# Narrow key products for the second step, halved copies in the first solve, and a new written-out order

## The chip, the cores and the metric

The kernel runs on one core of a Trainium2 chip. The metric is the device time of one execution in microseconds (us). The kernel before takes 895.24 us (median of 3 runs, 893.12 to 896.49). The core has five instruction streams that run beside each other and wait for each other by semaphores: PE (TensorE: matrix products and transposes, into PSUM banks), DVE (VectorE), ACT (ScalarE), POOL (GpSimd) and SP (which issues the DMAs). Each stream runs its own instructions in the order in which the program gives them.

## The reference

Three layers follow one another.

```
attention (B=4, H=8, S=768, D=48), a delta rule with one 48x48 state per batch and head:
    k_n = k / (|k| + 1e-6)
    for t in range(S):
        y[t]  = q[t] @ state
        state = state + beta[t] * outer(k_n[t], v[t] - state^T k_n[t])
x = y as [3072 tokens, 384]
first MoE-like layer:   h = x @ w_in (384 -> 2048);  g = relu(h)^2;  x = g @ w_out
second layer:           h = max(x @ w1, x @ w2, x @ w3) (384 -> 768);  out = h @ w_out2
```

## The kernel before

**Steps.** The 768 positions are cut into six steps of 128 (NS = 6, index t), each into two chunks of 64 positions (index c). In one step there are 16 pairs of heads (NP), so 32 units (NU: a pair and a chunk); a unit's two heads lie on partitions 0-63 and 64-127. Four batches (index b) of eight units make up a step.

**Per step** the kernel records these functions.

- `gram(t)`, line 464: for each batch the keys and the queries are transposed on PE (`features`) and copied from PSUM into the tile `W`; then `products` (line 483) multiplies each unit's keys with its keys (into bank `pk`) and with its queries (into bank `pq`). `pk` goes by ACT copies into the tile `G`; `pq` is multiplied by a triangular mask on DVE and goes back into `W`. For steps 1 and on the banks come from a ring of two (`gram_ring`), so that the transposes of the next batch wait until the copies and masks of this one have emptied the banks.
- For step 0 a key product is made as two products of 32 columns, one of them with its halves exchanged (`turned`), so that everything lands where `solve` wants it and one copy does (line 505). For the later steps it is one product of 64 columns, and up to four further small copies on ACT bring the quarters to their places (lines 506 to 511).
- `solve(t)`, line 551: from `G` a triangular inverse for each unit. DVE transposes `G` into `L`, runs two recurrences of 16 steps each (some 120 small dependent operations, tiles `T`, `Tn`), and transposes the result back into `Tn` and `G`. PE then makes two rounds of 32-by-32 products: `pm` (line 618), copied by ACT into `M1` (which is named L in the profile), and `pa`, `pb` (lines 629, 630). ACT copies these into `G` (line 635), ACT moves two blocks within `G` (line 638), and POOL clears the blocks from which they came (line 639).
- `chain(t)`, line 644: the recurrence over the two chunks, as alternating groups of small products and copies (`Removed`, `Updates`, `State`, `outputs`). `Updates` of chunk 0 in step 0 (line 677) is the first to read what `solve(0)` left in `G`.
- `moe1(t)`: the first layer for the step's 512 tokens, 16 blocks of `w_in` and `w_out`. In step 0 each weight block is also loaded and turned into a high and a low part (`load_w`: one DMA into one of two tiles `raw`, three operations on ACT and five on DVE through one tile `word`). `hidden` has one PSUM bank (`h_ring`), which ACT empties into `r`.

After the last step the second layer runs; it is not touched.

**Order.** Nothing is issued when it is recorded. A `Recorder` numbers every operation (products inside `together()` share a number) and `issue()` (line 229) emits them in the order of a list of numbers, `ORDER`, which has three parts: steps 0 to 4 with attention (3464 numbers), the end of the first layer (534) and the second layer (640). An engine's stream is what is left of the list when the other engines' numbers are struck out. So where an operation stands in the list decides what it can hold up on its own engine. Since `record` makes all calls, every row of the profile has line 247; rows are told apart by their tiles. A product of full 32-bit operands shows as two matmul instructions.

Of the kernel before, what the change touches and what calls it, by code (L numbers as in the profile page):

```python
# [11 lines left out]
AF = mybir.ActivationFunctionType  # L12
# [240 lines left out]
def kernel(  # L253
# [26 lines left out]
    pl = Recorder(nc)  # L280
# [183 lines left out]
    def gram(t):  # L464
# [66 lines left out]
        for keys in ((True, False) if t == 0 else (True,)):  # L531
            for b in range(B):
# [6 lines left out]
                nb = t * B + b + 2  # L539
                if nb < BLOCKS * B:  # L540
                    load_tok(nb // B, nb % B)
                products(slice(u0, u0 + 2 * HP), True, True)
        if t == 0:
            for b in range(2):
                load_tok(1, b)
# [494 lines left out]
```

## Time and profile before

| what | value |
|---|---|
| median of the runs | 895.24 us (893.12 to 896.49) |
| profiled execution | 894.54 us, span 892.8 us |
| PE busy | 858.6 us, 96% of the span |
| DVE busy | 535.7 us, 60% |
| ACT busy | 451.5 us, 51% |
| POOL busy | 35.0 us, 4% |
| mean granted TensorE clock | 0.965 of full speed |

The shares are means over stages with different limits. Slice by slice the page shows PE at six to nine tenths and at about half clock in the first four slices of 40 (the first 90 us), and at nine tenths or more and full clock in nearly all of the rest; DVE is at nine tenths or more in the first six slices except the first. The stretches in which PE waits are therefore to be looked for in the first 150 us.

### The profile page before, as it was taken

What the parts mean: (1) busy time and instruction counts of PE and PEld (TensorE: products, weight loads), DVE (VectorE), ACT (ScalarE), POOL (GpSimd) and SP (SyncE); (2) the same over time, 40 slices, a digit from 0 to 9 for tenths busy, and PEclk for the clock granted to TensorE, in tenths of its full rate; (3) what the DMA queues carried; (4) which work ended last, traced back from release to release, by engine and by line L of the source; (5) the groups of instructions that cost most, each with busy time, mean ns of one, the idle gap of its engine ahead of it and who ended that gap; (6) DMA issues with size and microseconds to landing.
All of it is one profiled execution on the core that took longest, in us unless ns stands there. A gap on an engine that the chain in (4) does not pass through costs nothing.

```text
span 892.8 us, 23837 instructions
## 1 busy us (share of the span) xinstructions
PE 858.6 (96%) x10284; PEld 717.2 (80%) x10284; DVE 535.7 (60%) x1185; ACT 451.5 (51%) x792; POOL 35.0 (4%) x55
## 2 busy tenths in 40 slices
PE   6678989999999999999999999999999999999998
PEld 4557976788887888888778888888988889898987
DVE  4999988799799689679543886325323141413131
ACT  5478778964655754665556896532222121312111
POOL 5010001000100100100000000000000000000000
PEclk8557999999999999999999999999999999999999
DMA  8456766576376347433434774420101000000000
GB/s 191 99 150 167 243 220 164 113 193 154 68 161 146 75 125 163 116 92 106 105 101 143 246 256 172 156 89 1 60 11 45 28 1 36 1 36 1 36 1 36
DMA packets 159785, 96.02 MB, mean 108 GB/s; under 512 B 129984, under 2 KB 133184, under 8 KB 159680
## 3 DMA queue, kind: packets, MB, share of 16 engines
q1 hardware_dynamic: 159168, 94.40, 38.3%
q8 instruction: 80, 1.31, 0.6%
q0 software_dynamic: 512, 0.10, 0.1%
q14 instruction: 25, 0.20, 0.1%
HBM read 79.53 MB, written 14.94 MB: 106 GB/s over the span
## 4 chain that ended last, share of the span: by engine, by line
PE 90%; DVE 6%; ACT 2%; DMA 1%; issue 1%; POOL 0%; SPq 0%; DVEq 0%; POOLq 0%; ACTq 0%
PE ps L247 90%; DVE Tn L247 1%; DVE word L247 1%; DMA raw<-in_moe_w_out_dram 1%; DVE W L247 1%; DVE T L247 1%; ACT G L247 0%; DMA kt<-in_k_dram 0%; ACT wo L247 0%; DVE wo L247 0%; ACT word L247 0%; DVE raw L247 0%; DVE L L247 0%; DVE US L247 0%; POOL G L247 0%
## 5 line engine op out<-in xcount | busy, mean ns | idle before, releaser
L247 PE MATMUL ps<-gh,wo 128*128 128x512 f32 (+1 forms) x624 | 161.4, 377 | 0.0
L247 DVE TENSOR_TENSOR r<-r,ps 128x512 f32<-128x512 f32 x72 | 49.4, 687 | 168.4 <-PE ps L247 167.9
L247 ACT ACTIVATE r<-ps 128x512 f32<-128x512 f32 (+1 forms) x140 | 80.0, 572 | 126.1 <-PE ps L247 122.6
L247 PEld LDWEIGHTS ps<-gh,wo 128*128 128x128 f32 x624 | 111.1, 188 | 21.0
L247 PE MATMUL ps<-xh,wih 128*128 128x512 f32 (+1 forms) x312 | 121.1, 388 | 4.2 <-ACT r L247 3.8
L247 PE MATMUL ps<-xh,wil 128*128 128x512 f32 (+1 forms) x312 | 116.6, 374 | 0.0
L247 PE MATMUL ps<-xl,wih 128*128 128x512 f32 (+1 forms) x312 | 116.5, 373 | 0.0
L247 DVE TENSOR_TENSOR gl<-r,gh 128x512 fp32r<-128x512 f32 (+1 forms) x104 | 66.6, 642 | 59.3 <-ACT gh L247 58.7
L247 PE MATMUL ps<-gl,wo 128*128 128x512 f32 (+1 forms) x312 | 83.4, 375 | 0.0
L247 PEld LDWEIGHTS ps<-xh,wih 128*128 128x128 f32 x312 | 58.6, 188 | 17.3 <-ACT r L247 5.6
L247 PEld LDWEIGHTS ps<-xl,wih 128*128 128x128 f32 x312 | 58.7, 188 | 10.8
L247 PEld LDWEIGHTS ps<-xh,wil 128*128 128x128 f32 x312 | 58.8, 188 | 9.0
L247 PEld LDWEIGHTS ps<-gl,wo 128*128 128x128 f32 x312 | 56.0, 188 | 10.7 <-DVE gl L247 0.3
L247 ACT ACTIVATE gh<-r 128x512 fp32r<-128x512 f32 (+1 forms) x104 | 61.6, 596 | 4.0 <-PE ps L247 1.8
L247 ACT ACTIVATE r<-r 128x512 f32<-128x512 f32 (+1 forms) x104 | 62.0, 597 | 2.4
L247 ACT ACTIVATE G<-ps 32x256 f32<-32x256 f32 (+3 forms) x116 | 51.3, 448 | 22.8 <-PE ps L247 21.0
L247 PE MATMUL ps<-W 64*64 64x64 f32 (+1 forms) x1664 | 49.3, 249 | 5.6 <-ACT W L247 3.5
L247 DVE TENSOR_TENSOR T<-T,Tn 128x96 f32<-128x96 f32 (+21 forms) x186 | 50.7, 273 | 2.1
L247 PEld LDWEIGHTS ps<-W 64*64 64x64 f32 (+1 forms) x1664 | 40.3, 151 | 13.6 <-issue 6.0
L247 ACT ACTIVATE raw<-ps 128x384 f32<-128x384 f32 (+1 forms) x32 | 16.5, 516 | 63.2 <-PE ps L247 63.1
L247 DVE TENSOR_TENSOR Tn<-L,T 128x96 f32<-128x96 f32 (+21 forms) x186 | 44.7, 271 | 0.8
L247 ACT ACTIVATE m1h<-r 128x512 fp32r<-128x512 f32 x18 | 11.4, 632 | 66.6 <-DVE r L247 66.6
(151 smaller groups left out, 1714.0 us busy)
## 6 DMA issues: line engine op xcount, KB each, us to landing
wo<-wod SPq DMA_DIRECT2D x88, 384.0 KB, 3.9
raw<-in_moe_w_out_dram SPq DMA_DIRECT2D x11, 768.0 KB, 5.4
raw<-in_moe_w_dram SPq DMA_DIRECT2D x9, 768.0 KB, 4.6
raw<-in_moe_w_in_dram SPq DMA_DIRECT2D x8, 768.0 KB, 5.0
wod<-wo SPq DMA_DIRECT2D x8, 768.0 KB, 5.4
out_dram<-raw SPq DMA_DIRECT2D x24, 192.0 KB, 1.8
x2d<-raw SPq DMA_DIRECT2D x12, 256.0 KB, 3.0
kn<-in_k_dram SPq DMA_DIRECT2D x14, 192.0 KB, 4.5
```

Of the source, the lines that this page charges most:

```text
L247: self.plan.add(lambda: fn(*args, **kw))
```

## The change

Four edits.

1. Step 1's key products are made as step 0's: two of 32 columns each in place of one of 64. The small copies behind them are not made in step 1.
2. In step 1 `products` is called twice per batch, first for the keys and then for the queries, so that a unit's key products and query products have numbers of their own and each group has its own bank and can stand anywhere in the order.
3. At the end of `solve`, the copies of `pa` (chunk 0) come ahead of those of `pb`; in step 0 the move within `G` and the clearing behind it are made chunk by chunk, four halves in place of two wholes.
4. The first two parts of `ORDER` are replaced (3484 and 534 numbers); the third is the same.

```diff
 ORDER = [
-29 32 4 0 24 28 1 27 25 26 5 30 2 3 1096 22 8 35 36 1119 37 38 7 49 324 39 50 51 52 40 167 53 163 63 64 41 21 42 43
...
-115 9 0 127 139 1 3 2 108 4 12 5 109 110 6 116 111 118 7 117 120 112 8 121 10 122 18 113 11 119 151 123 13 130 124
...
+115 0 9 139 1 3 2 4 108 151 5 109 127 110 6 118 111 116 7 117 120 112 8 121 10 122 18 113 11 119 123 13 128 12 163
...
@@ products
-                        if keys and t == 0:
+                        if keys and t < 2:
                             lo, hi = key[:, 0:32], key[:, 32:64]
                             turned = bass.AP(hi.tensor, hi.offset, [list(hi.ap)[0], [-32, 2], [1, 32]])
                             for o0, lhs, rhs in ((0, lo, key), (32, hi, turned)):
...
             if keys:
                 pl.scalar.activation(Gu, pk, AF.Copy)
-                for p0 in (32, 96) if t else ():
+                for p0 in (32, 96) if t > 1 else ():
                     p = slice(p0, p0 + 32)
                     pl.scalar.activation(Gu[p, :, 0:32], pk[p, :, 32:64], AF.Copy)
...
@@ gram
-                products(slice(u0, u0 + 2 * HP), True, True)
+                for which in ((True, False), (False, True)) if t == 1 else ((True, True),):
+                    products(slice(u0, u0 + 2 * HP), *which)
@@ solve
         Gc = G.rearrange("p (n c) k -> p c n k", c=2)
-        for p0 in (0, 64):
-            for c, px in enumerate((pa, pb)):
+        for c, px in enumerate((pa, pb)):
+            for p0 in (0, 64):
                 p = slice(p0, p0 + 32)
                 pl.scalar.activation(Gc[p, c, :, 32:64], px[p], AF.Copy, scale=-1.0)
-        for p0 in (32, 96):
-            p = slice(p0, p0 + 32)
-            pl.scalar.activation(G[p, :, 32:64], G[p, :, 0:32], AF.Copy)
-            pl.gpsimd.memset(G[p, :, 0:32], 0.0)
+        for cs in (slice(0, 1), slice(1, 2)) if t == 0 else (slice(0, 2),):
+            for p0 in (32, 96):
+                p = slice(p0, p0 + 32)
+                pl.scalar.activation(Gc[p, cs, :, 32:64], Gc[p, cs, :, 0:32], AF.Copy)
+                pl.gpsimd.memset(Gc[p, cs, :, 0:32], 0.0)
```

What the new list says of the first 135 us, read number by number against the recorded operations:

- **PE.** Ahead of the last key product of step 0 stand 16 transposes, where 18 stood. The products of step 1 come in alternating groups of four to sixteen narrow key products and two to eight query products. Counted by the shape of the part of the array that a product uses (all of it, 64 by 64, 64 by 32, 32 by 32), neighbours of unlike shape meet 68 times before the first `pm` product (35 before the change), 20 times from there to the first `Updates` product (11), and 28 times from there to the first product of `moe1` (24). Between the first `pm` product and the first `Updates` product stand 44 products of step 1's gram matrices (32 before); four query products of step 1 stand behind the first `Updates` product.
- **DVE.** The operations between the transpose into `L` and the transpose into `G` of step 0 are the same but for one more (a `word` operation of `load_w` that stood just ahead). Two masks of step 0's queries move forward in it. Between step 1's third and fourth pair of masks (in the profile those that begin at 50.09 and 57.15 us) stand a few more operations of the recurrence.
- **ACT.** The four halves of the move within `G` stand right behind the copy into `M1`; then come a copy of `G` for step 1, the `wih` copy of a weight block, and the two copies of `pa`. Near 130 us the squaring of `r` stands ahead of the `word` operation of the next weight block instead of behind it.
- **SP.** Step 0's queries and step 1's tokens are asked for earlier, step 0's values and chain keys later.

## Rows read from the trace of the kernel before

**Rows 1.** Busy time in stretches: window, us, PE, PEld, DVE, ACT, POOL, clock, DMA

```profile
17.75:60.51 42.76, 26.30 (x364) 20.54 (x364) 41.89 (x128) 23.86 (x43) 0.00 (x0) 0.54 0.60 143
60.51:71.32 10.81, 8.12 (x326) 6.51 (x324) 10.40 (x13) 8.00 (x13) 5.10 (x5) 0.50 0.37 113
71.32:80.20 8.88, 8.88 (x214) 8.13 (x214) 8.59 (x27) 7.60 (x15) 0.00 (x0) 0.50 0.55 171
80.20:120.00 39.80, 39.56 (x646) 37.65 (x641) 38.28 (x118) 30.09 (x66) 0.00 (x0) 1.00 0.71 208
120.00:150.00 30.00, 26.25 (x530) 20.58 (x532) 24.93 (x41) 23.32 (x38) 3.46 (x4) 1.00 0.60 187
150.00:893.00 743.00, 737.74 (x7954) 615.50 (x7946) 406.01 (x848) 349.25 (x607) 13.42 (x18) 1.00 0.34 94
```

**Rows 2.** What PE waited for over the span: us, times, longest

```profile
PE ps L247 <- DVE W L247: 9.8, 4, 3.3
PE ps L247 <- ACT r L247: 3.8, 4, 2.0
```

**Rows 3.** Timeline of PE, the last key products of step 0

```profile
15.37 1.71 PE L247 MATMUL ps<-W 64*32 64x64 f32 x53 [1.88 <-issue]
17.01 0.47 PE L247 MATMUL ps<-ident,r 128*128 128x128 f32 x1
```

**Rows 4.** Timeline of DVE, the solve of step 0

```profile
15.76 0.55 DVE L247 TENSOR_SCALAR word<-word 128x768 f32<-128x768 f32 x1
17.75 1.91 DVE L247 STREAM_TRANSPOSE L<-G 128x1024 f32<-128x1024 f32 x1 [1.44 <-ACT G L247]
...
57.15 0.64 DVE L247 TENSOR_TENSOR W<-ps,mask 64x512 f32<-64x512 f32 x1
...
58.53 1.98 DVE L247 STREAM_TRANSPOSE G<-T 128x1024 f32<-128x1024 f32 x1
```

**Rows 5.** ACT's groups by shape, 36 to 104 us: the small copies of step 1

```profile
L247 ACT ACTIVATE G<-ps 32x256 f32<-32x256 f32 x8 | 3.0, 375 | 0.2
...
L247 ACT ACTIVATE G<-ps 32x128 f32<-32x128 f32 x8 | 2.1, 263 | 0.1
```

**Rows 6.** Timeline of PE, one batch of step 1

```profile
50.84 0.90 PE L247 MATMUL ps<-ident,qt 128*128 128x128 f32 x3 [2.80 <-DVE W L247]
...
54.66 1.98 PE L247 MATMUL ps<-W 64*64 64x64 f32 x62 [0.61 <-ACT W L247]
```

**Rows 7.** Timeline of PE, products of unlike shape in turn

```profile
62.73 0.49 PE L247 MATMUL ps<-W 64*64 64x64 f32 x8
63.15 0.26 PE L247 MATMUL ps<-Tn,G 32*32 32x32 f32 x1
...
64.41 1.34 PE L247 MATMUL ps<-W 64*64 64x64 f32 x40
65.68 0.26 PE L247 MATMUL ps<-G,L 32*32 32x32 f32 x1
```

**Rows 8.** Timeline of PE, the end of solve(0) and the start of chain(0)

```profile
67.95 0.24 PE L247 MATMUL ps<-L,Tn 32*32 32x32 f32 x1
69.77 0.44 PE L247 MATMUL ps<-vn,G 64*64 64x48 f32 x2 [1.58 <-POOL G L247]
71.32 1.48 PE L247 MATMUL ps<-vn,G 64*64 64x48 f32 x23 [1.11 <-POOL G L247]
```

**Rows 9.** Timeline of ACT, and then of POOL, in the same stretch

```profile
69.69 0.91 ACT L247 ACTIVATE wih<-raw 128x768 fp32r<-128x768 f32 x1
70.63 1.20 ACT L247 ACTIVATE G<-ps 32x512 f32<-32x512 f32 x2
...
68.77 1.94 POOL L247 MEMSET G<- 32x1024 f32 x2 [0.61 <-ACT G L247]
```

**Rows 10.** Timeline of ACT, and then of PE, near 130 us

```profile
129.98 0.89 ACT L247 ACTIVATE word<-raw 128x768 f32<-128x768 f32 x1 [1.83 <-DMA raw<-in_moe_w_out_dram]
130.78 0.61 ACT L247 ACTIVATE r<-r 128x512 f32<-128x512 f32 x1
...
132.09 0.59 ACT L247 ACTIVATE r<-ps 128x512 f32<-128x512 f32 x1
...
132.74 0.50 PE L247 MATMUL ps<-xh,wih 128*128 128x512 f32 x1 [1.99 <-ACT r L247]
```

316 rows, old and new, of the table ORDER are left out of this document.

## The prediction

> **What bounds the kernel now.** First the busy time in stretches [rows 1], to see which engine fills which stretch. The reader is to see three regimes. From 17.75 to 120 us DVE is busy for 41.89 of 42.76 us, 10.40 of 10.81, 8.59 of 8.88 and 38.28 of 39.80: it is idle for only 0.9 + 0.4 + 0.3 + 1.5 = 3.1 us. PE is busy for 26.30 of 42.76 us in the first of these stretches, 8.12 of 10.81 in the second, and is full, with nothing to spare, from 71.32 to 120. From 120 to 150 PE is idle for 3.75 us. After 150 it is busy for 737.74 of 743 us: there nothing can be gained but by less work, and the change leaves none out. Then the waits of PE [rows 2]: what it waits for in front is DVE's masks (9.8 us in 4 times), and what it waits for later is ACT's `r` (3.8 us in 4 times). Then the timelines, at the places that the new list touches [rows 3 to 10]. The end is thus set by a chain: `solve(0)` on DVE, 17.75 to 60.51; its last products and copies on PE and ACT, to 71.32; PE to 120; and near 130 us the loading of weights, where ACT's `word` operation waits 1.83 us for a transfer, the copies of `r` stand behind it, and PE waits 1.99 us for `r` [rows 10].
>
> **The change part by part.**
>
> *The copies that go.* Eight of 375 ns and eight of 263 ns [rows 5], 5.1 us of ACT. ACT is busy for 23.86 of 42.76 us there [rows 1] and none of the four long waits of PE in that stretch is for it [rows 2]. I take 0; the ends are -5.1 (every one on the path) and 0.
>
> *The key products doubled.* 32 units times two heads are 64 more products, 128 more matmul instructions. What one costs comes from two runs of alike products: 8 between neighbours of another shape took 0.42 us (62.73 to 63.15) and 40 took 1.27 us (64.41 to 65.68) [rows 7]. So one costs (1.27 - 0.42)/32 = 0.027 us, and the rest, 0.21 us, comes once in each group, that is, once per change of shape. The last group of step 0, 53 in 1.64 us [rows 3], gives the same 0.027 with 0.2 left over. I take 0.19 a change, the ends being 0.16 and 0.21.
>
> [...]
>
> Where the changes of shape lie decides. (a) Before the first `pm` product there are 33 more (68 for 35): 6.3 us, and most of the instructions, on an engine that idles for 16.5 us in that stretch [rows 1]. They cost nothing as long as each batch is ready when DVE comes to its mask. The third batch is the tightest: PE restarts at 50.84 [rows 6] and the last query product comes some 5.8 us later; DVE masks at 57.15 [rows 4]. With 11 of the new changes and 32 of the new instructions it grows by 2.1 + 0.9 us, less 1.1 us, which key products fill while PE waits for `W` (0.61 of it in the row at 54.66 [rows 6]): 7.7 us. DVE's slot is 6.4 us and becomes some 7.05 with the operations moved into it. DVE then stands for 0.65 us, and behind that mask is the rest of the recurrence and the transpose into `G` at 58.53 [rows 4], for which everything waits. Ends: 0, and 3.3 (the longest wait in front [rows 2]). I take +0.65. (b) Between `pm` and chain(0) there are 9 more changes and some 24 more instructions: 1.7 + 0.65 = +2.35 us of PE. (c) From there to `moe1` 4 more and some 8 instructions: +1.0.
>
> *The start of solve(0).* Two transposes fewer stand ahead of the last key product; one is 0.90/3 = 0.3 us [rows 6]. DVE's transpose into `L` waits through ACT for these products [rows 4]: -0.6. Ends: -1.9, if the stall of 1.88 us ahead of them, which no wait explains ("issue" [rows 3]), went too, and +1.9 if it came twice.
>
> *The moved word operation.* 0.55 us [rows 4] goes from ahead of `solve(0)`, where DVE waits 1.44 us anyway, into it, where DVE is full: +0.55. The ends are 0 and 0.55.
>
> *The halves.* Before, the last `pa` product ends at 68.19 and chain(0) starts at 71.32 [rows 8], 3.13 us later, since ACT does the `wih` copy (69.69, 0.91 us) ahead of the last copies of `pa` and `pb` (70.63, 0.60 each), and POOL clears for 1.94 us [rows 9]. After, two copies of `pa` stand behind the product, 1.2 us and some 0.2 of passing on, with POOL's halves (0.49 each) beside them: 1.4, that is -1.7. The cover is the `wih` copy's being over by then; it now stands ahead of both copies. If it starts as late as 69.69, `pa` is copied by 71.8: +0.5, the other end.
>
> *The order near 130.* The squaring of `r` (0.61 us) ahead of the `word` operation that waits for a transfer [rows 10]: -0.6. Ends: -2.0, PE's whole wait, and 0.
>
> *The end of the first layer.* Another order of PE in a stretch where it is full [rows 1]: 0, within the 5.3 us that it idles after 150.
>
> The sum has two strands. PE alone would come to 120 us later by 2.35 + 1.0 - 1.7 = 1.65 us, beyond what DVE brings. But from 120 to 150 it idles for 3.75 us because the weights aren't there, and these are DVE's and ACT's work, which a late PE doesn't delay: the 1.65 are hidden. What isn't hidden is what moves DVE and the weights: -0.6 + 0.55 + 0.65 - 0.6 = 0.0. On the profile's 894.54 us (a span of 892.8 and 1.7 around it) that gives 894.6. The median of the runs is 0.7 above the profile, the lowest run 1.4 below it, so I add nothing.
>
> **The rivals.**
>
> *A. Faster: the front moves as a whole.* The stall of 1.88 us ahead of the last key products goes with the changed instruction stream, the tail of `solve(0)` gets its -1.7, and PE's wait near 130 gives 0.6: -4.2, 890.3. For it: the stall has no releaser in the trace [rows 3], and what starts `solve(0)` earlier moves DVE and the weights alike. Against it: the gain of the tail is PE's alone and would end in the wait for weights.
>
> [...]
>
> [...]
>
> *C. Slower: the drains outrun DVE's slots.* With 0.21 us a change and no key product that fills PE's wait for `W`, a batch of step 1 takes 5.8 + 2.3 + 0.9 = 9.0 us against a slot of 7.05, and DVE stands for 1.95 us at the last masks of each of three batches: +5.9, less the 0.65 that the sum has: 899.8, and with `pa` copied late (+0.5 instead of the tail's gain, PE then coming 3.9 us late to the 3.75 us of idling) 900. It decides as soon as a batch is over 7.05 us. For it: PE already stands at the masks (9.8 us [rows 2]) in a fixed cycle, each engine waiting in turn for the other. Against it: that PE waits there for DVE and not DVE for PE.
>
> *D. The change does nothing that the end sees*: both strands hidden, 895.2, the median.
>
> **How the numbers follow.** Forecast 0.36, D 0.12 (the two give no measurable change), A 0.16, B 0.14, C 0.22. About 0.5%, 4.5 us, is what a measurement of this kernel can tell from no change: faster is below 890.8, slower above 899.7. A and B lie just over that bound and would each fall short of it by a third of an us less, but with parts of the tail's or the start's gain beside them they reach 888; so I count 0.29 faster of their 0.30, and 0.21 slower of C's 0.22, whose miss goes to no change: 0.50. The likeliest one's own range comes from the ends of start (-1.9 for -0.6), order (-2.0 for -0.6) and DVE's wait (3.3 for 0.65): 892 to 897.5. To hold 8 in 10 the range takes in most of A and B (with the start's other end beside B, 890.1 - 1.3, about 888.5) and C to 900.5.
>
> **What would show it.** Right: no 32x256 and 32x128 copies of `G` in step 1; no idle DVE over 0.7 us ahead of a mask from 17 to 58; the transpose into `L` about 0.6 earlier and that into `G` within 1 us of 58.53; from the last 32-by-32 product to the first of `vn,G` some 1.4 us; PE full to 120 and then idle for about 2 us, in place of 3.75, up to 150. [...] DVE waiting for PE's products ahead of masks, two or three times over 1.5 us, says C. The forecast is wrong if PE's waits from 120 to 150 don't shrink when PE comes late, for then the weights hang on PE after all, and the 1.65 us count in full.

## The result and the profile after

The changed kernel takes 900.64 us (median of 6 runs, 898.0 to 903.07) beside 895.03 us for the kernel before (median of 6): 1.0063 times as long, 95% interval 1.0049 to 1.0078. A second set of runs of the same kernel (a_again, below) gave 899.58 us and 1.0050, 1.0033 to 1.0067. Slower, where no measurable change was forecast, and just outside the range of 888.5 to 900.5. The profiled execution has a span of 896.3 us; it is the quickest of the six (898.0 us), so its 3.5 us over the profile before are less than the medians' 5.6.

First, busy time cut at the same four events in both kernels: the transpose into `L`, the transpose into `G`, the second group of `vn,G` products (chain(0) under way), the first product of `moe1`, the end. Columns as in [rows 1]. The kernel before:

```profile
17.75:58.53 40.78, 24.34 (x353) 19.03 (x353) 39.91 (x128) 22.63 (x41) 0.00 (x0) 0.54 0.58 142
58.53:71.32 12.79, 10.08 (x335) 8.02 (x335) 12.37 (x14) 9.22 (x16) 5.10 (x5) 0.50 0.45 120
71.32:82.03 10.71, 10.47 (x287) 9.41 (x287) 10.03 (x32) 9.00 (x17) 0.00 (x0) 0.59 0.46 143
82.03:892.82 810.79, 801.96 (x9036) 672.45 (x9036) 467.78 (x1000) 401.26 (x707) 16.88 (x22) 1.00 0.37 103
```

The kernel after:

```profile
15.36:58.41 43.05, 32.97 (x447) 22.80 (x447) 40.65 (x128) 20.51 (x32) 0.00 (x0) 0.62 0.68 149
58.41:71.51 13.10, 11.92 (x352) 8.99 (x353) 12.14 (x15) 7.73 (x14) 3.40 (x6) 0.50 0.39 113
71.51:84.58 13.07, 11.83 (x295) 10.28 (x295) 11.04 (x25) 8.79 (x15) 2.25 (x3) 0.52 0.35 96
84.58:896.29 811.71, 802.59 (x9039) 674.08 (x9036) 468.85 (x1006) 396.90 (x706) 17.84 (x22) 1.00 0.38 103
```

`solve(0)` starts 2.4 us earlier, and loses 2.3 of them before it ends (43.05 for 40.78). The next stretch is 0.3 longer, the one to the first layer 2.4 longer, all the rest 0.9: together 3.5. PE is busy for 8.6 us more in the first stretch, DVE for only 0.7 more; so DVE has come to wait there. The timeline of DVE shows for whom (beside [rows 4], where no such wait stands):

```profile
15.36 1.93 DVE L248 STREAM_TRANSPOSE L<-G 128x1024 f32<-128x1024 f32 x1
...
36.64 0.68 DVE L248 TENSOR_TENSOR W<-ps,mask 64x512 f32<-64x512 f32 x1 [0.45 <-PE ps L248]
...
56.99 1.39 DVE L248 TENSOR_TENSOR W<-ps,mask 64x512 f32<-64x512 f32 x2 [1.06 <-PE ps L248]
58.41 1.94 DVE L248 STREAM_TRANSPOSE G<-T 128x1024 f32<-128x1024 f32 x1
```

PE in turn waits less for DVE's masks than the 9.8 us of [rows 2]; over the whole span it is now

```profile
PE ps L248 <- DVE W L248: 4.1, 3, 3.0
```

PE at the end of `solve(0)` and in chain(0), to be read beside [rows 8]:

```profile
69.90 0.24 PE L248 MATMUL ps<-L,Tn 32*32 32x32 f32 x1
70.90 0.41 PE L248 MATMUL ps<-vn,G 64*64 64x48 f32 x2 [0.76 <-POOL G L248]
71.51 1.91 PE L248 MATMUL ps<-vn,G 64*64 64x48 f32 x30 [0.20 <-POOL G L248]
74.66 1.94 PE L248 MATMUL ps<-vn,G 64*64 64x48 f32 x32 [1.24 <-issue]
```

The tail from the last `pa` product (ended at 70.14) to the chain is 1.37 us, as forecast. Then PE stands for 1.24 us in the midst of one group, for nothing that the profile names. The waits of PE from the first product of `moe1` to the end, columns as in [rows 2], before and after:

```profile
PE ps L247 <- ACT r L247: 3.8, 4, 2.0
```

```profile
PE ps L248 <- issue: 3.4, 5, 1.4
PE ps L248 <- ACT r L248: 1.2, 2, 0.7
```

The waits for `r`, 2.6 us of which the new order does away with, have been replaced by five that have no releaser. Before, there was one such wait, ahead of `solve(0)` [rows 3].

### The profile page after: what moved, and what is told of

Its sections match the earlier page's. It is cut to its first block, busy times and chain, and to the rows that moved or that the text cites. A ratio compares the mean times of both kernels' runs of the same rounds, so it can differ in the third digit from the quotient of the medians.

```text
span 896.3 us, 24087 instructions
## 1 busy us (share of the span) xinstructions
PE 869.6 (97%) x10412; PEld 724.6 (81%) x10412; DVE 537.8 (60%) x1185; ACT 443.3 (49%) x779; POOL 36.2 (4%) x57
## 4 chain that ended last, share of the span: by engine, by line
PE 93%; ACT 2%; DVE 2%; DMA 2%; issue 1%; SPq 0%; POOL 0%; ACTq 0%; DVEq 0%
PE ps L248 93%; DMA raw<-in_moe_w_in_dram 1%; DMA wod<-wo 1%; DVE W L248 1%; ACT W L248 1%; DMA wo<-wod 0%; ACT raw L248 0%; DVE G L248 0%; DVE L L248 0%; SPq L248 0%; ACT word L248 0%; ACT G L248 0%; ACT r L248 0%; ACT L248 0%; DVE Tn L248 0%
## 5 line engine op out<-in xcount | busy, mean ns | idle before, releaser
L248 PE MATMUL ps<-gh,wo 128*128 128x512 f32 (+1 forms) x624 | 163.4, 377 | 0.5 <-DMA wo<-wod 0.3
L248 PEld LDWEIGHTS ps<-gl,wo 128*128 128x128 f32 x312 | 55.9, 188 | 10.4
L248 PE MATMUL ps<-W 64*64 64x64 f32 (+1 forms) x1792 | 61.3, 251 | 2.5 <-ACT W L248 1.6
L248 ACT ACTIVATE G<-ps 32x256 f32<-32x256 f32 (+3 forms) x100 | 45.7, 469 | 31.4 <-PE ps L248 30.2
L248 PEld LDWEIGHTS ps<-W 64*64 64x64 f32 (+1 forms) x1792 | 46.5, 143 | 16.0 <-issue 8.8
L248 DVE TENSOR_TENSOR Tn<-L,T 128x126 f32<-128x126 f32 (+19 forms) x186 | 45.1, 271 | 0.9
L248 DVE TENSOR_TENSOR W<-ps,mask 64x512 f32<-64x512 f32 x48 | 33.0, 687 | 20.0 <-PE ps L248 19.3
```

Source lines behind the costliest of these rows:

```text
L248: self.plan.add(lambda: fn(*args, **kw))
```

## The experiments

Two theories at first. F: the waits without a releaser are waits for PE's own instructions. The traces have transfers of 16 KB each on an instruction queue, q8, here as the page of the profile after counts them (transfers, MB, share):

```profile
q8 instruction: 81, 1.33, 0.6%
```

That is one for each 128 of PE's 10412 matmul records or so. Each of the six waits begins within 2.1 us of the start of one, and ends 2.2 to 2.4 us behind that start. D: the loss is PE's added work, 64 products and the changes of shape. The pads move the instructions behind them against the blocks, at a place where PE waits anyway:

```diff
             for a in range(HP):
+                with pl.together():
+                    for _ in range(N if t == 0 and not keys and b == 0 and a == 0 else 0):
+                        pl.tensor.matmul(ps[0:32, 0, 0:64], ident[0:64, 0:32], ident[0:64, 0:64], start=True, stop=True)
                 pl.tensor.transpose(
```

**a_pad16, a_pad32, a_pad48** (N = 16, 32, 48).

> The changed kernel with 16 added products of 32 columns (32 matmul instructions more) at the first query transposes of step 0, where PE then waits 5 us anyway; they write a bank that the transposes overwrite. They move all later instructions of PE by 32 matmuls (and 32 weight loads) against the 16 KB blocks in which its instructions arrive. Theory F (fetches): the six waits of PE without a releaser in the profile after (4.6 us in all: 1.24 at 73.42, 1.41 at 141.13, 0.95 at 149.71 and three smaller; the kernel before has one, 1.88 at 13.49) are waits for such blocks, so they go or turn up at other work; their sum changes by over 1 us and the time with it (898 to 903). Theory D (drains): the loss is the 64 more products and the changes of shape; the waits without a releaser stay at the same work and the time at 900.6 within 0.7.

> As a_pad16 with 32 products (64 matmuls, half a block of 128). F: none of the six waits is left at the work where it was; a sum of such waits between 1 and 4 us elsewhere, and the time lower by what is missing to 4.6 (and by some 2 us more if the one at 73.42 goes, since the clock then rises earlier): 896 to 900. D: the same six waits, 900.6 within 0.7.

> As a_pad16 with 48 products (96 matmuls). F: the waits at other work again, the time differing from that of a_pad16 or a_pad32 by over 1 us. D: 900.6 within 0.7, as the others.

Measured: 911.23 us (1.0183 of before, 1.0159 to 1.0207), 902.81 (1.0099, 1.0082 to 1.0116) and 903.41 (1.0096, 1.0080 to 1.0112). D's 900.6 fails. F's direction holds and its sizes fail: the pads of 32 and 48 made it slower, not quicker, and a_pad16 left its range (its waits without a releaser come to 9.5 us, one of them 2.58 in chain(0), the clock was at half for two more stretches behind them, the mean over its profile 0.959 for 0.968, and POOL held DVE up, below). What speaks most for F is where the waits stand. Counting PE's matmul records from the start, the changed kernel stands without a releaser ahead of records 1112, 2260, 2388, 2643, 3026 and 5064. a_pad16, with 32 records more in front, stands ahead of 1113, 2260, 2388 and 3026 and four later ones; a_pad32, with 64 more, of 2260, 2388, 2516 and 2771 and others. Behind 130 us the counts stay, whatever the pad, and are multiples of 128 apart, but for a shortfall that grows to 21 by record 7871 (taken for records that the trace lacks); the work that stands there is another. Not every wait without a releaser is one of these. In chain(0), a_pad32 stands for 0.49 us ahead of record 1208, which is out of this step: there PE goes on at 75.64, 0.1 us behind the end of ACT's copy into `US`, which the next product reads.

**a_wide**: the four small copies stand right behind each copy of the bank.

```diff
-                        if keys and t < 2:
+                        if keys and t == 0:
...
-                for p0 in (32, 96) if t > 1 else ():
+                for p0 in (32, 96) if t else ():
```

> The changed kernel with step 1's key products of 64 columns again and the small copies on ACT back, each right behind the copy of its bank, all else in the new order. That takes out 128 matmul instructions, exactly one 16 KB block with their weight loads, so that from step 1's end on the blocks begin at the same work as in the changed kernel. D: the 3.5 us of instructions and the changes of shape that narrow products bring go, 896 or less. F: the waits at 141, 150 and 174 us stay, and the time falls by no more than 2 us: 898.5 to 901.

897.93 us (1.0041, 1.0025 to 1.0056), below F's range and above D's: both are in it. With 128 matmuls less the late waits stand ahead of records 2132, 2260, 2515 and 2898, 128 less each, and so at the same work: of the changed kernel

```profile
142.54 0.21 PE L248 MATMUL ps<-L,Tn 32*32 32x32 f32 x1 [1.41 <-issue]
150.66 0.62 PE L248 MATMUL ps<-W 64*64 64x64 f32 x25 [0.95 <-issue]
```

and of a_wide

```profile
143.68 0.21 PE L281 MATMUL ps<-L,Tn 32*32 32x32 f32 x1 [1.87 <-issue]
151.24 0.62 PE L281 MATMUL ps<-W 64*64 64x64 f32 x25 [0.36 <-issue]
```

**b_pad32, b_pad64**: the same in the kernel before, with products of 32 by 32 on the four diagonal blocks of `ident`; half a block and a whole one.

> The kernel before with 32 added products of 32 by 32 (64 matmuls, half of a 16 KB block of PE's instructions) ahead of the first query transpose of step 0, where PE waits 1.95 us for a transfer and DVE bounds the stretch. Their output is overwritten. Theory F (fetches): the kernel before has but one wait for a block because of where its blocks happen to begin; moved by half a block, it gets waits without a releaser behind 130 us as the changed kernel has, always at the same places in the count of matmuls, 1.5 to 8 us in all: 897 to 903. Theory D (drains): nothing has changed that costs: 894.6 within 0.7.

> As b_pad32 with 64 products (128 matmuls, a whole block), so that behind the pad the blocks begin at the same work as in the kernel before. F: no wait without a releaser behind 130 us, and what the pad itself costs is hidden or under 1.5 us: 894 to 896.5, below b_pad32 although it does twice as much. D: 894.6 to 896.5, and not below b_pad32.

903.06 us (1.0092, 1.0077 to 1.0106) for half a block, 895.05 (0.9997, 0.9988 to 1.0007) for a whole one, though the whole one is twice the work. From the first layer's start on PE waited in b_pad32

```profile
PE ps L247 <- issue: 6.1, 6, 1.4
PE ps L247 <- ACT r L247: 3.9, 4, 2.1
```

and in b_pad64

```profile
PE ps L247 <- ACT r L247: 4.8, 5, 2.2
PE ps L247 <- issue: 1.7, 1, 1.7
```

F is shown, for the waits and for what they cost here. Not all of its expectation came true: one wait of 1.7 us did come in b_pad64, and b_pad32 came just above its range. Besides its 6.1 us, the clock fell to half there for 3.4 us at 134 us, right behind a wait of 2.09 us for `r`; that is some 1.7 us more, if PE's work there would have taken half the time at full clock (an estimate).

**a_front, a_pool, a_front_pool, a_front_pool_wide, b_rest**: lists put together from the two. a_front is the changed kernel up to the first product of `moe1` and the old order from there; a_pool has POOL's first operations in their old order; the next two add these up, the last with wide products; b_rest is the old order up to that product and the new one from there. Of a_pool, POOL's numbers in the list (167, 168 and 34 clear `T`, `Tn` and `US`, the others issue transfers of beta):

```diff
-4 7 6 5 16 10 8 168 15 17 9 19 13 14 12 167 11 34 18
+4 7 6 5 167 16 10 8 15 17 9 19 13 14 12 11 18 168 34
```

> The changed kernel up to the first product of the first layer in the list; from there on, and in the list's second part, the order of the kernel before. All four edits of the code stay. The block phase is that of the kernel before (exactly one block more). F: the waits at 141, 150, 160 and 174 us (3.1 us) go, since other work stands where the blocks end there, the one at 73 stays: 896 to 898.5. D: the loss is made in the front and stays: 899.5 to 901.5.

> The changed kernel with POOL's operations of the first 14 us in the order of the kernel before: the clearing of T right behind the fourth transfer of beta, Tn and US last. The trace of a_pad16 shows a word operation of DVE that takes 4.1 us instead of 0.56, up to the end of POOL's clearing (14.16), and solve(0) starting 3.3 us late for it; in the profile after the same operation ended 0.6 us ahead of that clearing. Theory P: this is hit in a part of the runs of the changed kernel and makes their spread (898.0 to 903.1): here 898 to 899, and within 2.5 us of each other. Rival: POOL's order does nothing: 900.6 within 0.7, with the same spread.

> a_front with POOL's first operations in the order of the kernel before (as a_pool). F and P: no wait for a block behind 130 us, and no run in which solve(0) starts 3 us late; what is left is the front of the profile after, some 2.5 us late at the first layer for the wait at 73 us and the 9 more changes of shape ahead of chain(0): 896 to 897.5. If the order behind the front were no cause: 898.5 to 900.

> a_front_pool with key products of 64 columns in step 1 (as a_wide). Of the change that leaves the front's order, the separate banks and the halves. D's part, the price of the narrow products themselves, is the difference to a_front_pool: 1.5 to 3 us; so 893.5 to 895.5. If narrow products cost nothing: as a_front_pool.

> The kernel before up to the first product of the first layer in the list, and from there on (and in the second part) the order of the changed kernel; no edit of the code. F (fetches): the phase of the blocks is a whole block off that of the changed kernel, so the waits without a releaser at 141 to 174 us of its profile turn up here at the same work, 2.5 to 4.5 us: 897 to 900. D (the loss is in the front): 894 to 896.

Measured: a_front 899.54 us (1.0061, 1.0043 to 1.0080), a_pool 898.93 (1.0045, 1.0028 to 1.0062), a_front_pool 899.34 (1.0052, 1.0038 to 1.0066), a_front_pool_wide 897.0 (1.0032, 1.0020 to 1.0043), b_rest 894.87 (1.0003, 0.9991 to 1.0015). F's waits came and went where it said: none behind 80 us in a_front, 3.0 us in b_rest, at the work where the changed kernel has them. But F's times failed in both: b_rest is not slower, a_front hardly quicker. a_front_pool came where the rival to F and P had it. a_front_pool_wide missed its 893.5 to 895.5, but is 2.3 us under a_front_pool, inside D's 1.5 to 3; a_wide is 2.7 under the changed kernel. By the ratios the two differences are 1.8 and 2.0 us, with intervals that overlap a little. So narrow products make some 2 us in this front, and some 3 are left without them. From the first layer on the two orders take the same (811.71 and 810.79 us above, 812.35 in a_front_pool), the one with waits for blocks, the other with waits for `r`. The loss is ahead of the first layer. Of a_front_pool, again cut at the four events:

```profile
16.07:61.82 45.75, 35.70 (x447) 24.56 (x447) 40.66 (x128) 20.42 (x32) 0.00 (x0) 0.53 0.60 138
61.82:74.94 13.12, 11.93 (x353) 9.00 (x354) 12.15 (x15) 7.75 (x14) 2.84 (x5) 0.50 0.40 111
74.94:87.70 12.76, 11.45 (x295) 9.89 (x295) 10.60 (x25) 8.80 (x15) 2.64 (x3) 0.54 0.49 123
87.70:900.05 812.35, 802.78 (x9038) 672.68 (x9036) 468.93 (x1006) 401.62 (x706) 16.90 (x22) 1.00 0.37 102
```

and DVE in its `solve(0)`:

```profile
38.87 0.68 DVE L290 TENSOR_TENSOR W<-ps,mask 64x512 f32<-64x512 f32 x1 [1.68 <-PE ps L290]
...
49.54 0.69 DVE L290 TENSOR_TENSOR W<-ps,mask 64x512 f32<-64x512 f32 x1 [1.20 <-PE ps L290]
...
60.40 1.39 DVE L290 TENSOR_TENSOR W<-ps,mask 64x512 f32<-64x512 f32 x2 [1.10 <-PE ps L290]
```

In the five profiles with the old front and its products, pads and new late order included, the transpose into `G` starts 40.75 to 40.78 us behind that into `L`, DVE idle for 0.86 or 0.87 of them. In those with the new front it is 42.9 to 45.8, DVE idle for 2.2 to 5.1, mostly at masks. The new front leaves PE little slack there, so what PE's clock does in it now counts: DVE's idle time was 5.1 us where the granted clock of that stretch was 0.53 (a_front_pool), 3.9 to 4.0 at 0.55 and 0.56 (a_front, a_again, a_pad16), 3.5 at 0.59 (a_pool), 2.4 at 0.62 (after), 2.2 at 0.67 and 0.72 (a_pad32, a_pad48), while the kernel before ran at 0.54 with 0.9. With wide products it was 2.9 at 0.53 (a_front_pool_wide) and 2.5 at 0.56 (a_wide), so at like clock the narrow products are 1.4 to 2.2 us of it. All this goes with the wider spread of the runs; that it makes it is argued, not shown.

P (POOL) is a third thing. The new list moves POOL's first operations too, which the reading of the list ahead of the prediction left out. In a_pad16, timeline of DVE, then of POOL:

```profile
9.90 4.67 DVE L248 TENSOR_SCALAR word<-word 128x768 f32<-128x768 f32 x2 [7.84 <-ACT word L248]
```

```profile
11.04 0.97 POOL L248 MEMSET T<- 128x1024 f32 x1
11.94 0.62 POOL L248 DMA_DIRECT2D bl<-in_beta_dram  x1
12.55 1.61 POOL L248 MEMSET US<- 128x1792 f32 x1
```

The two `word` operations take 1.16 us where POOL's clearing comes behind them. Here the second (10.50 to 14.57) was running when the clearing of `T` began, and ended 0.4 us behind that of `US`; `solve(0)` began at 18.63 for 15.36. The operation was held so too in a_front (the two 4.68 us, `solve(0)` at 19.01) and in a_group (4.70 us, 18.16), and with POOL's old order in none. In all three the long operation lies beside two clearings and the issue between them and ends 0.4 us behind the second clearing, though here the one held had started first (10.50 for 11.04). No run shows what holds it. Not every operation of DVE is held: in the profile after, `SCALAR_TENSOR_TENSOR` (10.53, 0.96 us) ran as long as ever (28 of them take 0.95 in the mean) beside the clearing of `T` (11.07 to 12.04). There a `word` operation takes 1.63 us in chain(0) instead (72.60 to 74.23), beside POOL's clearings of `US` and `Tn` (71.96 to 73.81). a_pool's times don't show that P makes the changed kernel's spread: 895.8 to 901.2 is as wide as before.

**b_halves**: the old kernel with the halved copies of `solve(0)` alone (the loop over `cs` in the diff of the change). In the list both copies of `pa` stand ahead of `wih`: ACT's and POOL's numbers there, those of the halves in brackets,

```diff
-316 ... 314 ... 310 315 wih 317 312 311 ... 313
+[314 316] ... [318 320] ... 310 312 [315 317] wih [319 321] 311 ... 313
```

> The kernel before with the halved copies and clearings of solve(0) alone, both copies of pa ahead of the wih copy; PE's instructions are the same, so its blocks are too. The prediction's two strands: the tail from the last pa product to the first Updates group that follows on its clears shrinks from 3.1 to about 1.5 us, chain(0) starts 1.6 us earlier, and PE's waits between 120 and 150 us grow by as much: 894.2 to 895.5. Rival: PE's gain counts in full: 893.3.

895.06 us (1.0009, 0.9999 to 1.0019), as the two strands have it. But not by their reason: PE stood as long as ever near 130 us (2.00 us for `r`). The tail went from 3.1 to 2.4 us only, and the first layer began at 80.63, as in b_rest (80.75), for which the tail is the old one: the gain was lost within chain(0) (11.1 us from its second group to the first layer, 10.4 in b_rest).

**a_group, b_alt, b_sep, a_again**: what makes the batches too long, changes of shape (S) or the places (O)? b_alt has the first edit of the change alone, b_sep the first two, both in the old order. In a_group the key (K) and query (Q) products of a batch change places, as in the second batch:

```diff
-K K K K Q K K Q Q K Q Q Q Q K Q
+K K K K K K K K Q Q Q Q Q Q Q Q
```

> The changed kernel with the same places in the list for step 1's products, but in each batch the eight units' key products first and the eight units' query products behind them: some 7 changes of shape fewer in the second and third batch each, and fewer in the fourth; the number of products and everything else is the same. Theory S (slots: DVE stands in solve(0) because a batch of step 1 takes PE longer than DVE's work between two pairs of masks): a batch gets 1.3 us shorter, DVE's waits for products in solve(0) (2.4 us in the profile after, up to 5.1 in other runs of this front) fall under 1.5, 897.5 to 899.5. Rival O (the places of transposes and copies set these waits, not the changes of shape): 900.6 within 0.7.

> The kernel before with narrow key products in step 1 and without the small copies behind them, in its own order: each unit then runs two narrow products, a query product, two narrow ones, a query product, so a batch has 32 changes of shape more instead of 11 and 32 instructions more. S: 32 x 0.19 + 0.9 = 7.0 us more for a batch, 12.8 against a slot of 6.4: DVE stands for some 6 us at each of the last three pairs of masks, solve(0) takes 55 to 60 us instead of 40.8, 908 to 916. O, or a change of shape that costs less than the rows of the kernel before let it seem: under 900.

> b_alt with key and query products of a batch apart: eight units' keys, then eight units' queries, in the places where the old order has the units. Two changes of shape more a batch: 0.4 + 0.9 us, 7.1 at most against 6.4. S: solve(0) takes 41 to 43 us, 894.5 to 897. O: as b_alt, or as the kernel before within 0.7.

> The changed kernel once more, for a second profile. If its loss and its spread are made ahead of the first layer, the stretch from the first product of the first layer to the end is 811 to 813 us as in all kernels with blocks in this phase (810.8 in the profile before), and that product begins at 84 to 88 us, later by what solve(0) takes beyond 43 us. If they are made behind it: over 814.

a_group 897.7 us (1.0029, 1.0011 to 1.0047), b_alt 930.27 (1.0405, 1.0388 to 1.0423), b_sep 895.94 (1.0018, 1.0002 to 1.0034). DVE's waits for PE from 15 to 86 us, in a_group, b_alt and b_sep:

```profile
DVE W L281 <- PE ps L281: 1.7, 1, 1.7
```

```profile
DVE W L279 <- PE ps L279: 27.4, 3, 9.2
```

```profile
DVE W L280 <- PE ps L280: 3.2, 2, 2.3
```

b_alt shows the mechanism: the old order with alternating shapes, and DVE stands for 9 us at each of three pairs of masks; 6 were expected, so the price was taken too low. From the transpose into `G` to the last `pa` product PE took 17.2 us there for 7.7, which makes most of the rest of its 35. (In b_alt narrow key products also stand between the two heads' query products, where one of the same shape stood; the runs don't part the two.) b_sep's time is in S's range, its profile is not: 44.0 us for the 41 to 43 from transpose to transpose. But that profile is of a run of 900.23 us, 4 above its median, as a_group's (901.84) and a_front's (904.3) are of their slowest runs.

In a_group the waits at the later masks are gone, and one stays, of 1.7 us, at the first mask of step 1. a_wide, without narrow products, has it too, and so has b_sep, in the old places:

```profile
37.75 0.68 DVE L281 TENSOR_TENSOR W<-ps,mask 64x512 f32<-64x512 f32 x1 [1.64 <-PE ps L281]
```

```profile
43.73 0.68 DVE L280 TENSOR_TENSOR W<-ps,mask 64x512 f32<-64x512 f32 x1 [2.29 <-PE ps L280]
```

So it is S for the later batches; for the first the runs don't decide, since a_wide's wait could be O's and b_sep's S's. What a_group, a_wide and b_sep share is the second edit, which takes a batch's query products apart from its key products. The traces show a price for that which neither theory counted. At half clock, 4, 8 and 16 query matmuls in a row take 0.41, 0.62 and 1.05 us in the profile after (from 52.02, 53.78 and 55.76): 0.053 each beside what the group pays once. In [rows 7], where key and query products of 64 columns take turns, one costs 0.027. For the 32 query matmuls of a batch that is 0.8 us (an estimate). No run has the second edit alone, so that it makes the first wait is argued.

By time a_group and a_again overlap. a_again's profile has the transpose into `G` 44.57 us behind that into `L`, waits of 1.70 and 1.07 us at masks, the first layer at 84.97 and 812.48 us from there: as expected for a loss made in front.

No kernel of the study is quicker than the kernel before.

## Why the prediction was wrong

*Right, by its steps.* No run shows a gain from the copies that go: b_sep has none of them and isn't quicker, though it has the narrow products as well. From the end of the transpose into `G` to the last `pa` product PE took 9.8 us for 7.7: +2.1, forecast +2.35. The tail lost 1.76 us, forecast 1.7. The moved `word` operation is 0.5 us in `solve(0)`. From chain(0) to `moe1`, at like clock (0.63), PE is busy for 10.9 us (a_again) for 9.9 (b_rest): +1.0, as forecast. The later order costs nothing measurable (b_rest).

*The start of solve(0)* was mis-sized, in the changed kernel's favour: -2.4 us for -0.6 (-1.3 and -1.4 beside b_halves and b_rest, which have the same front and start at 16.67 and 16.76). The stall ahead of the last key products went, as rival A had it, and all of it was lost again.

*"I take +0.65" for DVE's wait at the masks* failed in size. It counted one batch, the third. The rows show waits at two or three pairs of masks: 1.5 us in the profile after, 2.8 in a_again, 4.0 in a_front_pool. That is the mechanism of rival C, at a fourth to two thirds of its 5.9. What the sum missed is that PE's waits for the masks, 9.8 us in four [rows 2], were about all the slack that there was for 8.6 us more of busy PE; that this slack changes with the clock (DVE idle for 5.1 us at 0.53 and for 2.2 at 0.67); and that query products set apart cost 0.053 us a matmul. It priced every matmul at 0.027, read where key and query products take turns [rows 7]. That changes of shape cost time, b_alt shows: 27.4 us of waits in three batches, each with 32 changes more. What rival C and theory D call drains is the price of a change, 0.21 us by [rows 7]; no run shows what TensorE does at one. What makes the some 3 us that the new front loses with wide products too stays open.

*"The 1.65 are hidden" failed.* PE's lateness is not absorbed near 130 us. a_front_pool begins the first layer 5.7 us later than the kernel before, with the old order behind it, and still waits 0.5, 0.5 and 2.0 us for `r` between 125 and 140. So what ACT and DVE load hangs on how far PE is, as the prediction's last sentence named it. From the first layer on every kernel of this study without a shifted block takes 810.6 to 814.8 us: what is late there is late at the end. By this the forecast's own front terms, -0.6 + 0.55 + 0.65 + 2.35 + 1.0 - 1.7 = +2.25, would have given some 897; the profile after is at 898.0, the medians at 899.6 and 900.6.

*A term was missing.* The one wait "issue" [rows 3] was taken for something that could go or come twice there. It was a wait for a block of instructions (it is gone in b_pad32, where the blocks are shifted), and the change, which moves other work to the blocks' ends, has six: 4.65 us, 1.24 of them in chain(0), where the clock rose at 84.08 us for 80.20 (that this wait put the rise off is the author's estimate). The 3.4 behind the first layer's start ate the 2.6 that the new order won on `r`. So the forecast's -0.6 near 130 was there, and more, and was spent.

*Rival B*, a clock that rises earlier, stands in the chances and in the range with 4.4 us (890.1), half of the 8.88 us that PE ran at 0.50 [rows 1]. No run shows this term. In b_pad64 the granted clock between the second `vn,G` group and the first layer was 0.83, in b_rest 0.63: 10.11 us for 10.41. That is 0.3 us less, where PE's work alone would have taken some 2.5 less (an estimate from the two clocks). That DVE is busy for 8.59 of those 8.88 us [rows 1] fits this; one pair of runs shows no more.

## What to carry to other kernels

Before a wait of one engine is taken for cover, ask what that engine's slack is in each slot and whether the slot's other engine is the bound; a cover of 2 us is gone when 3 us of work come under it, and the price is then the bound's. Read the price of a product where its neighbours are those that it will have. When PE runs long groups of small products, look for waits without a releaser just behind transfers on the instruction queue (here they ended 2.2 to 2.4 us behind the start of one): an edit that adds or moves instructions shifts the blocks, and a padded control (half a block, a whole block) tells that from the edit's own worth.

## What the runs showed of the hardware

Adding 64 small matmuls that nothing needs cost 8.1 us of 895 (b_pad32), and adding 128 cost nothing (b_pad64). The profile after has 81 transfers of 16 KB on the instruction queue, one for each 128 or so of PE's 10412 matmuls and as many weight loads. Six of them have a wait of PE without a releaser behind them, of 0.24 to 1.41 us, the others none. Waits over 1 us have products of 64 by 64 or less just ahead of them in the profiles after (1.24 and 1.41 us), before (1.88), of a_wide (1.87), of a_pad32 (1.76) and of a_pad16, which has the longest, 2.58 us (76.02 to 78.60).

Products of 64 by 64 cost 0.027 us a matmul at half clock where key and query products take turns [rows 7], and 0.053 where query products stand in a row (after, 4 in 0.41 us from 52.02 and 16 in 1.05 from 55.76). No run shows why.
